# Rewriting the tail of an attention and expert kernel: pointer operands, tables by matmul, rows scattered by register

## Chip, cores, metric

One Trainium2 chip, one core. The metric is the device time of one execution in microseconds (us). Times quoted for a kernel are medians of its runs. Of every run the span (first to last instruction, 1.8 to 2.1 us shorter than the device time) and the mean granted TensorE clock are on record; of one run of each kernel the whole trace is kept, called its profiled run below.

## The reference

LayerNorm, attention with 16 query heads that share one key and one value head, a residual, then a block that picks the 8 rows with the largest routing score, sends those through a gated expert and adds the result back to them.

```python
B, S, D, H, F, C = 1, 2048, 448, 16, 1792, 8
h  = x + softmax(q @ k.T * Dh**-0.5) @ v @ wo          # x normalised by LayerNorm first
xn = layernorm(h)
r  = xn @ w_r                                          # one routing score for each row
idx = argsort(-r)[:8]
y  = (silu(xn[idx] @ w_gate) * (xn[idx] @ w_up)) @ w_down * sigmoid(r[idx])
h2 = h + xn; h2[idx] += y
```

## The kernel before

Each operation is handed to a static scheduler (`G.op(engine, function, assumed ns, reads, writes, ...)`), which works out one fixed order for each engine before the program is built. `DV` is VectorE, `AC` ScalarE, `PO` GpSimd, `PE` TensorE, `SP` SyncE. `port=True` tells the scheduler to keep an operation from running beside GpSimd's operations of the same mark. `urgent`, `prio` and the assumed time steer the order.

The main part runs in 16 blocks of 128 rows. ScalarE computes most exponentials. The rest is shared by VectorE and GpSimd. At the end of each block come small VectorE operations on one value per row:

```python
G.op(DV, lambda e: e.scalar_tensor_tensor(st[:, t, 6:7], mv[:, t, 0:1], -1.0, st[:, t, 4:5],
                                          ALU.mult, ALU.mult), 80,
     reads=[("mv", t), ("st4", t)], writes=[("st6", t)])
# ... (cut)
G.op(DV, lambda e: e.scalar_tensor_tensor(r_col[:, t:t + 1], st[:, t, 6:7], sw[:, 0:1], st[:, t, 2:3],
                                          ALU.mult, ALU.add), 80,
     reads=[("st6", t), "sw", ("st2", t)], writes=[("r", t)], port=True)
```

When 15 of the 16 blocks have their routing scores, the candidates are gathered: 8 from each block, into a row of 120.

```python
G.op(DV, lambda e: e.tensor_copy(rp[:, 0:NT1], r_col[:, 0:NT1]), 80, reads=[...], writes=["rp"])   # the "rp cast"
G.op(PE, mm(ps[0:NT1, VB, 0:128], rp[:, 0:NT1], ident[:, :], True, True), 60, ...)
G.op(DV, lambda e: e.tensor_copy(r16[:, :], ps[0:NT1, VB, 0:128]), 200, ...)
G.op(DV, lambda e: e.max(c8[:, :], r16[:, :]), 200, ...)
dma(crow[0:1, :].rearrange("o (t k) -> o t k", k=8), c8[:, :], ["crow"], reads=["c8"])
G.op(DV, lambda e: e.max_index(i8[:, :], c8[:, :], r16[:, :]), 260, ...)
# ... (cut: row number of each candidate into i8f)
dma(cidx[:, :], i8f[:, :], ["cidx"], reads=["i8f"])
```

The last block and the expert follow. The expert's result is scattered by one indirect DMA. Every engine then loads a flag that says whether the fast path was numerically safe, and branches over a second, exact program:

```python
evs.append(G.op(PO, lambda e: e.indirect_dma_start(out=out[0],
    out_offset=bass.IndirectOffsetOnAxis(ap=idx2[:, 0:1], axis=0), in_=rows8, ...), 1000, ...))

def run(e):                                   # one for each engine
    G.emit(eng, e)
    e.wait_ge(G.flag_sem, G.flag_val)
    bad = e.value_load(flag[0:1, 0:1])
    with e.If(bad != 0):
        ...                                   # the exact program
    if eng == SP:
        for s, v in G.final_waits:
            e.wait_ge(s, v)
```

## Time and profile before

| | before |
|---|---|
| median of 3 runs | 393.55 us (392.94 to 394.22) |
| profiled run: device time, span, mean TensorE clock | 394.32, 392.5, 0.991 |
| last exponential ends | 370.8 us |
| from there to the end of the span | 21.7 us |

### The profile page before, as it was taken

To read this page: it belongs to the slowest core of one execution; us is meant where nothing else is said; L and a number is where in the kernel's file an instruction comes from. 1 tells how busy PE (TensorE), PEld (TensorE's weight loads), DVE (VectorE), ACT (ScalarE), POOL (GpSimd) and SP (SyncE) were. 2 spreads that over 40 slices of the span, in tenths; PEclk is the share of its full clock that TensorE was granted. 3 is DMA by queue.
4 is the path that set the end of the run, shared out by engine and by line. 5 is a ranking of instruction groups with operands and counts; after the bars stand their busy time and mean duration, and the time that the engine had idled before them with its cause. 6 is when DMAs were issued, how large, how long until landed. Compare 5 with 4: busy or idle time off the path is not lost.

```text
span 392.5 us, 8604 instructions
## 1 busy us (share of the span) xinstructions
PE 319.9 (82%) x3501; PEld 110.6 (28%) x3501; DVE 338.5 (86%) x695; ACT 366.7 (93%) x307; POOL 193.4 (49%) x180
## 2 busy tenths in 40 slices
PE   8899887878787888878787878888787878788794
PEld 4454322323232222223231322222232312122242
DVE  6995888989898998989898989989898989879872
ACT  5799999999999999999999999999999999799850
POOL 7410135646555464656365454646563654456410
PEclk9999999999999999999999999999999999799999
DMA  7993000010102010100102010100101020100110
GB/s 210 234 244 86 11 17 15 14 52 4 63 5 63 3 52 13 34 33 5 61 3 65 3 63 4 49 16 29 39 4 62 3 65 3 60 3 3 47 42 10
DMA packets 19892, 17.59 MB, mean 45 GB/s; under 512 B 6326, under 2 KB 17094, under 8 KB 19846
## 3 DMA queue, kind: packets, MB, share of 16 engines
q1 hardware_dynamic: 19781, 16.95, 15.8%
q8 instruction: 30, 0.49, 0.6%
q14 instruction: 17, 0.13, 0.1%
q0 software_dynamic: 64, 0.02, 0.0%
HBM read 11.44 MB, written 5.53 MB: 43 GB/s over the span
## 4 chain that ended last, share of the span: by engine, by line
DVE 60%; PE 23%; ACT 12%; issue 4%; POOL 0%; POOLq 0%
DVE Y L910 28%; PE ps L478 22%; ACT P L885 12%; DVE Y L919 11%; DVE st L752 2%; DVE Q L596 2%; DVE hbuf L730 2%; DVE Ot L932 2%; DVE junk L766 2%; DVE bn L734 2%; DVE bn L609 1%; DVE xnT L653 1%; DVE xx L638 1%; DVE mv L735 1%; DVE K L670 1%
## 5 line engine op out<-in xcount | busy, mean ns | idle before, releaser
L885 ACT ACTIVATE P<-ps 128x1536 bf16<-128x1536 f32 (+1 forms) x281 | 355.2, 1422 | 5.0 <-PE ps L478 4.5
L910 DVE TENSOR_SCALAR Y<-ps 128x512 int16<-128x512 f32 x240 | 164.0, 683 | 32.7 <-PE ps L478 32.6
L921 POOL TENSOR_TENSOR Y<-Y,step 128x1024 int32<-128x1024 int32 x60 | 113.5, 1892 | 142.7 <-DVE Y L919 142.1
L478 PE MATMUL ps<-Q,K 32*128 32x512 bf16 x1024 | 111.5, 385 | 62.6 <-DVE Y L910 45.8
L478 PE MATMUL ps<-Y,Vs 128*32 128x512 bf16 x960 | 89.6, 387 | 2.4 <-DVE Y L919 0.5
L478 PEld LDWEIGHTS ps<-Q,K 32*128 32x128 bf16 x1024 | 33.2, 91 | 177.8 <-ACT P L885 160.2
L919 DVE TENSOR_SCALAR Y<-Y 128x2048 int16<-128x2048 int16 x120 | 82.3, 696 | 0.6
L478 PE MATMUL ps<-P,Vs 128*32 128x512 bf16 x784 | 73.0, 388 | 0.0
L478 PE MATMUL ps<-zero 128*32 128x512 bf16 (+3 forms) x162 | 51.4, 395 | 1.2 <-DVE zero L497 1.2
L478 PEld LDWEIGHTS ps<-Y,Vs 128*32 128x32 bf16 x960 | 23.3, 94 | 33.3 <-issue 17.9
L713 POOL TENSOR_TENSOR On<-Ot,Rb 128x256 bf16<-128x256 f32 x28 | 19.8, 727 | 15.2 <-DMA Rb<-l_scr 15.2
L478 PEld LDWEIGHTS ps<-P,Vs 128*32 128x32 bf16 x784 | 18.8, 94 | 28.7 <-issue 26.7
L738 POOL TENSOR_TENSOR st<-st,nhalf 128x1 f32<-128x1 f32 x15 | 17.8, 1185 | 4.6 <-DVE st L736 4.6
L478 PEld LDWEIGHTS ps<-zero 128*32 128x32 bf16 (+1 forms) x162 | 14.4, 101 | 14.8 <-issue 7.5
L478 PE MATMUL ps<-xnT,wq_pad 112*128 112x128 bf16 x256 | 17.4, 220 | 0.0
L758 POOL TENSOR_SCALAR xx<-hbuf,st 128x448 bf16<-128x448 f32 x15 | 15.6, 1041 | 0.0
L478 PEld LDWEIGHTS ps<-xnT,wq_pad 112*128 112x128 bf16 x256 | 14.4, 98 | 3.6 <-issue 3.4
L478 PE MATMUL ps<-wo_pad,On 128*128 128x448 bf16 x64 | 15.0, 355 | 0.0
L755 POOL TENSOR_SCALAR xx<-hbuf,st 128x448 bf16<-128x448 f32 x15 | 11.2, 746 | 1.6
L730 DVE TENSOR_TENSOR hbuf<-ps,xx 128x448 f32<-128x448 f32 x15 | 9.4, 623 | 2.3 <-PE ps L478 2.3
L596 DVE TENSOR_SCALAR Q<-ps,qone 128x512 bf16<-128x512 f32 x15 | 11.2, 744 | 0.0
L752 DVE SCALAR_TENSOR_TENSOR st<-mv,st 128x1 f32<-128x1 f32 x15 | 11.1, 738 | 0.0
(179 smaller groups left out, 170.1 us busy)
## 6 DMA issues: line engine op xcount, KB each, us to landing
Rb<-l_scr SPq DMA_DIRECT2D x14, 256.0 KB
x_scr<-xx SPq DMA_DIRECT2D x15, 224.0 KB, 2.5
out_dram<-xx SPq DMA_DIRECT2D x16, 112.0 KB, 1.7
wg_sb<-in_B_w_gate_dram SPq DMA_DIRECT2D x1, 1568.0 KB, 14.3
wu_sb<-in_B_w_up_dram SPq DMA_DIRECT2D x1, 1568.0 KB, 20.5
wd_sb<-in_B_w_down_dram SPq DMA_DIRECT2D x1, 1568.0 KB, 25.4
xx<-in_A_x_dram SPq DMA_DIRECT2D x3, 448.0 KB, 5.5
wq_sb<-in_A_wq_dram SPq DMA_DIRECT2D x2, 196.0 KB, 2.9
```

The costliest lines, as they stand in the source:

```text
L478: return lambda e: e.matmul(o, lhsT=l, rhs=r, start=start, stop=stop)
L596: G.op(DV, lambda e: e.tensor_scalar(Q[:, q, :, :].rearrange("p g n -> p (g n)"), ps[:, bank, :], qone[:, 0:1], None, ALU.add), dvt(512), ...
L713: G.op(PO, lambda e, c=c: e.tensor_tensor(On[:, rb, c], Ot[:, rb, c], Rb[:, rb, c], ALU.mult), 750, reads=[both[h], rk[h]], writes=[("On", ...
L730: G.op(DV, lambda e: e.tensor_tensor(hbuf[:, hr, :], ps[:, bank, 0:D], x_sb[:, t, :], ALU.add), dvt(D), reads=[pk(bank), ("x", t)], writes ...
L738: G.op(PO, lambda e: e.tensor_tensor(st[:, t, 4:5], st[:, t, 7:8], nhalf[:, 0:1], ALU.pow), 600, reads=[("st7", t), "nhalf"], writes=[("st ...
L752: G.op(DV, lambda e: e.scalar_tensor_tensor(st[:, t, 6:7], mv[:, t, 0:1], -1.0, st[:, t, 4:5], ALU.mult, ALU.mult), 80, reads=[("mv", t), ...
L755: G.op(PO, lambda e: e.tensor_scalar(outf[:, t, :], hbuf[:, hr, :], st[:, t, 5:6], st[:, t, 6:7], ALU.mult, ALU.add), 800, reads=[("h", hr ...
L758: G.op(PO, lambda e: e.tensor_scalar(xn[:, t, :], hbuf[:, hr, :], st[:, t, 4:5], st[:, t, 6:7], ALU.mult, ALU.add), 800, reads=[("h", hr), ...
L885: G.op(AC, lambda e: e.activation(P[:, s0:s0 + w, :], ps[:, b0:b0 + w, :], ACT.Exp, bias=-(ZERO + SHIFT) * OCT, scale=OCT), w * 427 + 50, ...
L910: G.op(DV, lambda e: e.tensor_scalar(Y[:, y, 0, q, :].bitcast(I16), ps[:, vb, :], 0.0, 32639.0 - STEP[3], ALU.max, ALU.min), dvt(512), rea ...
L919: done = [G.op(DV, lambda e, c=c: e.tensor_single_scalar(y[c].bitcast(I16), y[0].bitcast(I16), STEP[c], ALU.add), 600, reads=r, writes=[(" ...
L921: G.op(PO, lambda e: e.tensor_tensor(y[3].bitcast(I32), y[0].bitcast(I32), step3[:, 0:1].broadcast_to([128, 1024]), ALU.add), 2050, reads= ...
```

## The change

The intent has three parts. The small VectorE operations that read two tensors become `tensor_scalar` with a per-row pointer operand, which is meant to keep GpSimd from holding them (the `st6` operations took 0.738 us each on average before). The two candidate tables are made by a masked multiply and a matmul with ones instead of by two DMAs. The eight result rows are stored by eight DMAs whose row number is in a register, four from SyncE and four from ScalarE, instead of one indirect DMA from GpSimd. With it go a longer assumed time for one matmul group (700 ns, was 250) and the copy of the base rows on ScalarE. The core of the diff (cut: the same rewrite in three more places, set-up of the masks, new reads and writes):

```diff
-        G.op(DV, lambda e: e.scalar_tensor_tensor(st[:, t, 6:7], mv[:, t, 0:1], -1.0, st[:, t, 4:5],
-                                                  ALU.mult, ALU.mult), 80,
+        G.op(DV, lambda e: e.tensor_scalar(st[:, t, 6:7], mv[:, t, 0:1], st[:, t, 4:5], -1.0, ALU.mult, ALU.mult),
+             80,
...
-        dma(crow[0:1, :].rearrange("o (t k) -> o t k", k=8), c8[:, :], ["crow"], reads=["c8"])
+        G.op(DV, lambda e: e.tensor_tensor(spread, bmask, c8[:, :].unsqueeze(1).broadcast_to([NT1, NT1, 8]), ALU.mult),
+             200, reads=["c8", "bmask"], writes=["spread"])
+        G.op(PE, mm(ps[0:1, VB, 0:NC1], onesb[0:NT1, 0:1], wq_sb[0:NT1, 3, 0:NC1], True, True), 60, mode="F",
+             reads=["onesb", "spread"], writes=[pk(VB)])
...
-                  mm(ps[0:8, VB, 26:27], trow[:, 0:8], oneF[:, 0:1], True, True)], 250, mode="F",
+                  mm(ps[0:8, VB, 26:27], trow[:, 0:8], oneF[:, 0:1], True, True)], 700, mode="F",
...
+    def fetch(e, j0):
+        v = None
+        for j in range(j0, j0 + 4):
+            row[j] = e.value_load(idx2[0:1, j:j + 1], min_val=0, max_val=S - 1)
+        return row[j0]
+    loads = [G.op(q, lambda e, j0=j0: fetch(e, j0), 400, reads=["idx2"], writes=[("row", j0)], name="load",
+                  prio=hot + 70) for q, j0 in ((SP, 0), (AC, 4))]
...
-    G.op(DV, lambda e: e.tensor_copy(base8, ps[0:8, 2, 0:D]), 531, reads=[pk(2)], writes=["base8"])
+    post.append(G.op(AC, lambda e: e.activation(base8, ps[0:8, 2, 0:D], ACT.Identity), 480, reads=[pk(2)],
+                     writes=["base8"]))
...
-    evs.append(G.op(PO, lambda e: e.indirect_dma_start(
...
+    for j in range(8):
+        q, ld = (SP, loads[0]) if j < 4 else (AC, loads[1])
+        o = G.op(q, lambda e, j=j: e.dma_start(out[0, bass.ds(row[j], 1), :], rows8[j:j + 1, :]), 60,
...
```

More of the change, by code (lines that the diff above doesn't have):

```diff
@@ L343, in emit @@
             hold = None
-            if w and not o.dma:
+            if w and not o.dma and o.name != "load":
                 hold = w.pop()
@@ L431, in _main @@
     i8 = sb("i8", [NT1, 8], U32)
-    i8f = sb("i8f", [NT1, 8], F32)
     crow = sb("crow", [1, NC1], F32)
     cidx = sb("cidx", [NC1, 1], F32)
+    tbase = sb("tbase", [128, 1], F32)
+    tbi = sb("tbi", [128, 1], I32)
     top8 = sb("top8", [1, 8], F32)
@@ L453, in _main @@
     fin = wq_sb[0:8, 2, 176:180].bitcast(F32)
-    idx2 = wq_sb[0:8, 2, 180:182].bitcast(U32)
+    idx2 = wq_sb[0:1, 2, 180:196].bitcast(I32)
     selb = wq_sb[:, 0, 0:256].bitcast(F32)
@@ L458, in _main @@
     onesb = wq_sb[:, 1, 128:256]
+    spread = wq_sb[0:NT1, 3, 0:NC1].rearrange("p (t k) -> p t k", k=8)
+    bmi = wq_sb[0:NT1, 3, 0:2 * NC1].bitcast(I32)
+    spreadi = wq_sb[0:NT1, 3, 120:120 + NC1].rearrange("p (t k) -> p t k", k=8)
+    bmask = wq_sb[0:NT1, 3, 240:240 + NC1].rearrange("p (t k) -> p t k", k=8)
     wst = sb("wst", [128, 12], F32)
@@ L576, in _main @@
     G.op(PO, lambda e: e.tensor_copy(pcol[:, :], iota_ci[:, 0:1]), 150, reads=["iota_ci"], writes=["pcol"], prio=123)
+    G.op(DV, lambda e: e.tensor_single_scalar(tbi[:, :], iota_ci[:, 0:1], 120, ALU.bitwise_and), 70, reads=["iota_ci"],
+         writes=["tbi"], prio=123)
+    G.op(DV, lambda e: e.tensor_single_scalar(tbase[:, :], tbi[:, :], 16.0, ALU.mult), 70, reads=["tbi"],
+         writes=["tbase"], prio=123)
     G.op(PO, lambda e: e.tensor_copy(rsig[:, 0:1], iota_ci[:, NT - 1:NT]), 150, reads=["iota_ci"], writes=["rs0"],
          prio=123)
-    G.op(PO, lambda e: e.iota(iota_ci[:, 0:8], [[1, 8]], base=0, channel_multiplier=0), 140, reads=["pcol", "rs0"],
+    G.op(PO, lambda e: e.iota(iota_ci[:, 0:8], [[1, 8]], base=0, channel_multiplier=0), 140, reads=["pcol", "rs0", "tbi"],
          writes=["iota_ci"], prio=124)
@@ L582, in _main @@
     G.op(PO, lambda e: e.memset(xselT[:, :, :], 0.0), 250, writes=["xselT", ("wq_sb", 1)], prio=124)
+    G.op(PO, lambda e: e.iota(bmi, [[-1, NT1], [0, 8]], base=0, channel_multiplier=1), 250, reads=["xselT"],
+         writes=["bmask"], prio=124)
+    G.op(PO, lambda e: e.tensor_single_scalar(bmask, bmi.rearrange("p (t k) -> p t k", k=8), 0, ALU.is_equal), 560,
+         reads=["bmask"], writes=["bmask"], prio=124)
     G.op(DV, lambda e: e.tensor_reduce(sw[:, :], w_rb[:, :], AX.X, ALU.add), dvt(D), reads=["w_rb"], writes=["sw"],
@@ L743, in out_proj @@
                  reads=[("h", hr), "w_rb"], writes=["junk", ("st2", t)], port=True, prio=G.prio - 880)
-            G.op(DV, lambda e: e.scalar_tensor_tensor(st[:, t, 3:4], mv[:, t, 0:1], sw[:, 0:1], st[:, t, 2:3],
-                                                      ALU.mult, ALU.subtract), 80,
+            G.op(DV, lambda e: e.tensor_scalar(st[:, t, 3:4], mv[:, t, 0:1], sw[:, 0:1], st[:, t, 2:3],
+                                               ALU.mult, ALU.subtract), 80,
                  reads=[("mv", t), "sw", ("st2", t)], writes=[("st3", t)], **now)
@@ L768, in out_proj @@
              reads=[("h", hr), ("st4", t), "w_rb"], writes=["junk", ("st2", t)], port=True)
-        G.op(DV, lambda e: e.scalar_tensor_tensor(r_col[:, t:t + 1], st[:, t, 6:7], sw[:, 0:1], st[:, t, 2:3],
-                                                  ALU.mult, ALU.add), 80,
-             reads=[("st6", t), "sw", ("st2", t)], writes=[("r", t)], port=True)
+        G.op(DV, lambda e: e.tensor_scalar(r_col[:, t:t + 1], st[:, t, 6:7], sw[:, 0:1], st[:, t, 2:3],
+                                           ALU.mult, ALU.add), 80,
+             reads=[("st6", t), "sw", ("st2", t)], writes=[("r", t)])
     hot = -3000.0
@@ L791, in last_proj @@
              reads=[pk(bank), ("mv", t), "w_rb"], writes=["junk", ("st2", t)], port=True)
-        G.op(DV, lambda e: e.scalar_tensor_tensor(st[:, t, 3:4], mv[:, t, 0:1], sw[:, 0:1], st[:, t, 2:3],
-                                                  ALU.mult, ALU.subtract), 80,
+        G.op(DV, lambda e: e.tensor_scalar(st[:, t, 3:4], mv[:, t, 0:1], sw[:, 0:1], st[:, t, 2:3],
+                                           ALU.mult, ALU.subtract), 80,
              reads=[("mv", t), "sw", ("st2", t)], writes=[("st3", t)])
@@ L798, in last_proj @@
         G.prio = hot + 10
-        G.op(DV, lambda e: e.scalar_tensor_tensor(st[:, t, 6:7], mv[:, t, 0:1], -1.0, st[:, t, 4:5],
-                                                  ALU.mult, ALU.mult), 80,
+        G.op(DV, lambda e: e.tensor_scalar(st[:, t, 6:7], mv[:, t, 0:1], st[:, t, 4:5], -1.0, ALU.mult, ALU.mult),
+             80,
              reads=[("mv", t), ("st4", t)], writes=[("st6", t)])
@@ L948, in stage1 @@
         G.op(DV, lambda e: e.max(c8[:, :], r16[:, :]), 200, reads=["r16"], writes=["c8"])
-        dma(crow[0:1, :].rearrange("o (t k) -> o t k", k=8), c8[:, :], ["crow"], reads=["c8"])
+        G.op(DV, lambda e: e.tensor_tensor(spread, bmask, c8[:, :].unsqueeze(1).broadcast_to([NT1, NT1, 8]), ALU.mult),
+             200, reads=["c8", "bmask"], writes=["spread"])
+        G.op(PE, mm(ps[0:1, VB, 0:NC1], onesb[0:NT1, 0:1], wq_sb[0:NT1, 3, 0:NC1], True, True), 60, mode="F",
+             reads=["onesb", "spread"], writes=[pk(VB)])
         G.op(DV, lambda e: e.max_index(i8[:, :], c8[:, :], r16[:, :]), 260, reads=["r16", "c8"], writes=["i8"])
-        G.op(DV, lambda e: e.tensor_copy(i8f[:, :], i8[:, :]), 70, reads=["i8"], writes=["i8f"])
-        G.op(DV, lambda e: e.scalar_tensor_tensor(i8f[:, :], pcol[0:NT1, 0:1].broadcast_to([NT1, 8]), 128.0, i8f[:, :],
-                                                  ALU.mult, ALU.add), 80, reads=["i8f", "pcol"], writes=["i8f"])
-        dma(cidx[:, :], i8f[:, :], ["cidx"], reads=["i8f"])
+        G.op(DV, lambda e: e.tensor_tensor(spreadi, bmask, i8[:, :].unsqueeze(1).broadcast_to([NT1, NT1, 8]), ALU.mult),
+             200, reads=["i8", "bmask"], writes=["spreadi"])
+        G.op(PE, mm(ps[0:NC1, VB, 128:129], spreadi.rearrange("p t k -> p (t k)"), onesb[0:NT1, 0:1], True, True), 60,
+             mode="F", reads=["onesb", "spreadi"], writes=[pk(VB)])
+        G.op(DV, lambda e: e.tensor_copy(crow[:, :], ps[0:1, VB, 0:NC1]), 200, reads=[pk(VB)], writes=["crow"])
+        G.op(DV, lambda e: e.tensor_tensor(cidx[:, :], ps[0:NC1, VB, 128:129], tbase[0:NC1, :], ALU.add), 80,
+             reads=[pk(VB), "tbase"], writes=["cidx"])
         G.op(DV, lambda e: e.max(top8[:, :], crow[:, :]), 190, reads=["crow"], writes=["top8"])
@@ L1137, in _main @@
     G.op(DV, lambda e: e.tensor_copy(ohf[0:8, 1, :], oh[0:8, 1, :]), 70, reads=["oh1"], writes=["ohf1"])
-    G.op(PE, [mm(ps[0:8, rbank, 0:2], ohf[:, 0, :], rsig[:, :], True, False),
-              mm(ps[0:8, rbank, 0:2], ohf[0:8, 1, :], cols[:, 0:2], False, True)], 200, mode="F",
+    G.op(PE, [mm(ps[0:8, rbank, 0:1], ohf[:, 0, :], rsig[:, 1:2], True, False),
+              mm(ps[0:8, rbank, 0:1], ohf[0:8, 1, :], cols[:, 1:2], False, True),
+              mm(ps[0:1, rbank, 8:16], rsig[:, 0:1], ohf[:, 0, :], True, False),
+              mm(ps[0:1, rbank, 8:16], cols[:, 0:1], ohf[0:8, 1, :], False, True)], 400, mode="F",
          reads=["ohf0", "ohf1", "rs0", "rs1", "cols"], writes=[pk(rbank)])
-    G.op(DV, lambda e: e.tensor_copy(fin[:, :], ps[0:8, rbank, 0:2]), 130, reads=[pk(rbank)], writes=["fin"])
-    G.op(DV, lambda e: e.tensor_copy(idx2[:, :], fin[:, 0:1]), 70, reads=["fin"], writes=["idx2"])
+    G.op(DV, lambda e: e.tensor_copy(fin[:, 0:1], ps[0:8, rbank, 0:1]), 130, reads=[pk(rbank)], writes=["fin"])
+    G.op(DV, lambda e: e.tensor_copy(idx2, ps[0:1, rbank, 8:16]), 130, reads=[pk(rbank)], writes=["idx2"])
+    row = {}
+    def fetch(e, j0):
[5 more added lines that the diff above has]
+                  prio=hot + 70) for q, j0 in ((SP, 0), (AC, 4))]
     G.op(PE, [mm(ps[0:8, 2, 0:D], oh[:, 0, :], outf[:, t, :], True, False),
@@ L1145, in _main @@
          reads=["oh0", "oh1", ("outf", t), "both8"], writes=[pk(2)])
-    G.op(DV, lambda e: e.tensor_copy(base8, ps[0:8, 2, 0:D]), 531, reads=[pk(2)], writes=["base8"])
+    post.append(G.op(AC, lambda e: e.activation(base8, ps[0:8, 2, 0:D], ACT.Identity), 480, reads=[pk(2)],
+                     writes=["base8"]))
     G.prio = hot
-    G.op(DV, lambda e: e.scalar_tensor_tensor(rows8, ps[0:8, dbank, 0:D], fin[:, 1:2], base8, ALU.mult, ALU.add), 540,
+    G.op(DV, lambda e: e.scalar_tensor_tensor(rows8, ps[0:8, dbank, 0:D], fin[:, 0:1], base8, ALU.mult, ALU.add), 540,
          reads=[pk(dbank), "fin", "base8"], writes=["rows8"])
-    evs.append(G.op(PO, lambda e: e.indirect_dma_start(
-        out=out[0], out_offset=bass.IndirectOffsetOnAxis(ap=idx2[:, 0:1], axis=0), in_=rows8, in_offset=None,
-        bounds_check=S - 1, oob_is_err=False), 1000, reads=["rows8", "idx2"] + [("out", k) for k in range(NT)],
-        writes=["scatter"], dma=True))
+    for j in range(8):
+        q, ld = (SP, loads[0]) if j < 4 else (AC, loads[1])
+        o = G.op(q, lambda e, j=j: e.dma_start(out[0, bass.ds(row[j], 1), :], rows8[j:j + 1, :]), 60,
+                 reads=["rows8"] + [("out", k) for k in range(NT)], writes=[("scatter", j)], dma=True)
+        o.deps[ld.idx] = False
+        evs.append(o)
     G.prio = 7000
```

## The prediction

> **What bounds the kernel now.** I read the page first, by engine and by group, then ScalarE's waits stretch by stretch, then the timeline around the one large wait, then the tail by engine.

> The costliest group of the page, and the small VectorE operation that the change rewrites:

> ```profile
> L885 ACT ACTIVATE P<-ps 128x1536 bf16<-128x1536 f32 (+1 forms) x281 | 355.2, 1422 | 5.0 <-PE ps L478 4.5
> L752 DVE SCALAR_TENSOR_TENSOR st<-mv,st 128x1 f32<-128x1 f32 x15 | 11.1, 738 | 0.0
> ```

> ScalarE runs the softmax exponentials 355.2 us of 392.5 and idles only 5.0 us before them. From about 20 to 370.8 us the kernel is ScalarE-bound: time saved on VectorE counts there only where ScalarE waits. ScalarE's waits by stretch: 1.7 us at 14.5 to 20, 1.0 at 20 to 40, 0.3 at 40 to 80, none from 80 to 330, then 2.1 us in one event at 330 to 346. The timeline has its cause:

> ```profile
> 334.44 1.89 POOL L921 TENSOR_TENSOR Y<-Y,step 128x1024 int32<-128x1024 int32 x1
> 334.51 1.85 DVE L752 SCALAR_TENSOR_TENSOR st<-mv,st 128x1 f32<-128x1 f32 x1
> ...
> 336.28 0.68 DVE L910 TENSOR_SCALAR Y<-ps 128x512 int16<-128x512 f32 x1
> ...
> 337.10 0.40 PE L478 MATMUL ps<-Q,K 32*128 32x512 bf16 x4 [2.17 <-DVE Y L910]
> ...
> 337.54 4.04 ACT L885 ACTIVATE P<-ps 128x1536 bf16<-128x1536 f32 x3 [1.35 <-PE ps L478]
> ```

> A one-element operation takes 1.85 us because it ends when GpSimd's 1.89 us operation ends. The next VectorE score tile is late, TensorE waits 2.17 us for it, ScalarE 1.35 us. The windows view shows the after-effect (columns: busy time of PE, PEld, DVE, ACT, POOL with counts, TensorE clock, DMA share, GB/s):

> ```profile
> 330.00:334.50 4.50, 3.77 (x51) 1.08 (x43) 4.39 (x10) 4.50 (x4) 3.17 (x3) 1.00 0.03 5
> 334.50:337.50 3.00, 0.83 (x16) 0.20 (x12) 2.61 (x4) 1.69 (x2) 2.88 (x3) 1.00 0.00 0
> 337.50:345.30 7.80, 7.48 (x55) 1.42 (x59) 5.51 (x11) 6.86 (x6) 2.21 (x2) 0.56 0.25 79
> ```

> TensorE, nearly idle for 3 us, then runs at 0.56 of its clock for 7.8 us, and ScalarE waits 0.50 and 0.23 us more. The event costs 1.35 + 0.50 + 0.23 = 2.08 us. In 13 of the 15 blocks the same operation starts inside that GpSimd operation and ends with it; in twelve it takes about 0.75 us (0.68 in the first) and nothing waits.

> After the last exponential (370.78) the rest, 21.7 us, is a serial chain: accumulator copy, selector matmuls, Ln/Exp, normalise, output projection, LayerNorm and routing on VectorE, expert matmuls, combine, scatter. Any step there counts in full.

> [...]L752 (two inputs) is held, while L750, a 128x1 TENSOR_SCALAR issued 0.06 us before it under the same GpSimd operation, takes 0.14 us in all these blocks. [...]here about 3 us of near idleness led to 0.56. [...]Here one such load takes 0.49 us on SyncE and 0.47 on ScalarE; no run yet shows several in a row.

> **The change part by part.**

> A. Pointer forms, main part. Fifteen `st6` operations become TENSOR_SCALAR with one SBUF tensor and a pointer. A 128x1 TENSOR_SCALAR with a pointer takes 0.21 us (L747, L795); so VectorE saves (0.738 - 0.21) x 15 = 7.9 us, nearly all of it off the bound. What counts is the event: -2.1 us. The fourteen `r` operations (mean 0.222) gain almost nothing.

> B. Candidate tables. The row of 120 candidates leaves by a DMA issued at 369.44, landing 2.0 us later; the index table likewise from 370.52. A masked multiply (estimate 0.25 us from the 0.23 to 0.28 us of its like), a bf16 matmul with its hand-over (0.4) and a PSUM copy (0.24) give the row in about 0.9 us instead. VectorE idles 1.08 us before 371.57, so part of the top-8 search moves there. This chain ends in a gather that is not needed until 380.2, so its own speed is worth nothing. Its VectorE and TensorE work is, because it now sits in front of the critical chain:

> ```profile
> 373.77 0.41 DVE L716 TENSOR_TENSOR On<-Ot,Rb 128x256 bf16<-128x256 f32 x1
> 374.83 0.15 DVE L974 COPY cols<-ps 8x3 f32<-8x3 f32 x1 [0.64 <-PE ps L478]
> 374.91 0.14 DVE L976 COPY bc<-ps 128x8 f32<-128x8 f32 x1
> 374.98 0.40 DVE L716 TENSOR_TENSOR On<-Ot,Rb 128x256 bf16<-128x256 f32 x1
> ```

> The second On has its input at 374.35, yet stands behind two copies that wait for a group of small fp32 matmuls (374.12 to 374.80), which holds up the projection too. The static scheduler of the kernel thought this group took 250 ns; the change tells it 700, near the 0.68 measured. With earlier data and the right length it should put the group elsewhere: -0.6 us.

> C. Pointer forms, tail. `st6` and `st3` of the last block each take a pointer more, 0.06 to 0.1 us, on the serial VectorE chain 376.2 to 380.1: +0.15.

> D. Expert part. The base row copy moves to ScalarE:

> ```profile
> 382.77 0.69 DVE L1123 TENSOR_TENSOR Y<-ps,Y 128x224 bf16<-128x224 f32 x2 [0.62 <-PE ps L478]
> 383.38 0.60 DVE L1146 COPY Y<-ps 8x448 f32<-8x448 f32 x1
> 383.91 0.47 DVE L1127 COPY Y<-ps 112x256 bf16<-112x256 bf16 x2
> ```

> The transposes of the first half end at about 383.5; L1127, which feeds the down projection, starts at 383.91 behind L1146: -0.3 us. The index group becomes eight passes of small fp32 matmuls instead of four, just before the gate projection at 380.96: +0.1. Four register loads enter ScalarE's queue at about 381.4, before the Silu, which starts at 381.94 now. Silu's result has some 0.5 us of slack (ready 382.25, used 382.77). Four loads in series, 4 x 0.47 = 1.9 us, would cost about 1.0; overlapped ones nothing. I take +0.4.

> E. Scatter. Before:

> ```profile
> 387.55 0.67 DVE L1148 SCALAR_TENSOR_TENSOR Y<-ps,wq_sb,Y 8x448 bf16<-8x448 f32 x1 [2.92 <-PE ps L478]
> 389.22 0.92 POOL L1150 DMA_INDIRECT out_dram<-Y,wq_sb  x1 [11.52 <-DVE Y L1148]
> ```

> From the row result (388.22) 1.0 us passes to the start of the indirect DMA, and 2.8 more to its landing (392.0): 3.8 us. After it, each queue issues four DMAs. A DMA issue costs SyncE 0.32 to 0.34 us at best and 0.49 when it has only four rows; with address registers I take 0.45, so the last starts 1.4 us after the rows and lands 1.5 to 1.9 later, at about 3.1. But SyncE now does its end work after its last issue (1.8) rather than beforehand: flag load 0.49, branch 0.05, 0.46 to the first wait, and 24 final waits, two to an instruction at about 0.065, 0.8. That ends at 3.6, with 0.55 us per issue at 4.0. So the landing gains 0.7 and the end about 0: I take 0.0.

> F. Start. Two 0.15 us operations on VectorE and two on GpSimd (0.25, 0.6) fall into idle stretches: 0, or +0.1.

> Sum: -2.1 - 0.6 + 0.15 - 0.3 + 0.1 + 0.4 + 0.0 + 0.05 = -2.3 us; 393.55 - 2.3 = 391.25.

> **Rivals.** (1) The event does not come out, because a pointer read is held like a second tensor, or the rebuilt static schedule makes another of its kind, or it belongs to the profiled run (394.32, above the median 393.55). [...]for the second, that every order in the program is recomputed. Then only -0.2 remains, or +1: 393.3 to 394.5. (2) The register loads run in series before the Silu: -1.7 instead of -2.3, 391.9. (3) The scatter pays in full, because the single-row issues are cheap (0.33) and landing is what ends the run: -0.6 more, 390.6; with the loads hidden too, 390.2.

> **Range and chances.** A is the largest term and has about 0.8 of being real; B and D rest on an order that I have not seen. Together: 391.2, 8 times in 10 between 389.6 and 393.2. Two per cent is 7.9 us, more than everything that the tail could give back, and no part adds as much: within 2% at 0.96.

> **What would show it.** A: L752's successor at about 0.21 us in every block, no ScalarE wait between 80 and 346 us, TensorE clock 1.00 throughout. B: the second On starting within 0.1 us of its Exp. D: L1127 straight behind the transposes, Silu not behind loads. E: time from the row result to the last landing near 3.1 us, but the end of SyncE near 3.8. The prediction is wrong if a wait like that of 334.5 stands elsewhere, or if the tail from 370.8 on is longer than 21 us.

What the terms had besides the traces were estimates: that a pointer read would not be held (A; the trace had for it only L750, 0.14 us beside the GpSimd operation that held L752, and without a pointer), and that register loads might overlap (D, +0.4 between no cost and 1.0). "One such load" is the load of the flag, a register load: 0.490 us on SyncE and 0.467 on ScalarE in the kernel before.

## The result

| | before | after |
|---|---|---|
| median | 393.47 us (4 runs, 392.94 to 394.22) | 399.16 us (4 runs, 398.32 to 399.89) |
| profiled run: device time, span, clock | 394.32, 392.5, 0.991 | 398.32, 396.3, 0.981 |

The changed kernel is slower: ratio 1.0143, 95% interval 1.0116 to 1.0169. A ratio here is the mean time of one kernel's runs over that of the other's of the same rounds, so not quite the ratio of the medians. The result is within 2%, as the prediction gave 0.96 for, but 6 us above its upper end of 393.2.

Where the 3.8 us between the two profiled spans went, by the time from one step to the next:

| stretch | before | after | difference |
|---|---|---|---|
| start to end of the last exponential | 370.77 | 368.28 | -2.49 |
| to the copy of the last accumulator | 0.80 | 1.99 | +1.19 |
| to the LayerNorm statistics of the last block | 4.61 | 6.38 | +1.77 |
| to the gate projection | 4.77 | 5.17 | +0.40 |
| to the Silu | 0.99 | 3.14 | +2.15 |
| to the product of gate and up projection | 0.83 | 0.39 | -0.44 |
| to the down projection | 1.55 | 1.24 | -0.31 |
| to the rows' result | 3.90 | 3.96 | +0.06 |
| to the end | 4.29 | 5.74 | +1.45 |

The main part gained about as predicted, and four places lost more: two before the gate projection, the Silu and the end. The first row alone is good to about 1 us only: the last exponential ends at 366.24 us in the profiled run of ptr_rp and at 367.45 in that of ptr_rp_base, though VectorE, ScalarE and GpSimd do the same in the same order up to there. Below, "rows to end" is the last row of this table.

**The held operation moved.** The group view of the changed kernel (columns: busy us, mean ns) shows the rewritten operation free in all 15 blocks, and two others that are not:

```profile
L765 DVE TENSOR_SCALAR st<-mv,st 128x1 f32<-128x1 f32 x15 | 3.1, 205 | 0.0
L956 DVE CAST rp<-r_col 128x15 bf16<-128x15 f32 x1 | 1.9, 1904 | 0.0
L962 DVE TENSOR_TENSOR wq_sb<-wq_sb,c 15x120 bf16<-15x120 bf16 x1 | 0.5, 537 | 0.0
```

The timeline of the kernel before around its `rp` cast (columns: start, duration, engine, line, operation):

```profile
368.25 0.15 DVE L752 SCALAR_TENSOR_TENSOR st<-mv,st 128x1 f32<-128x1 f32 x1
368.32 0.17 DVE L943 CAST rp<-r_col 128x15 bf16<-128x15 f32 x1
...
368.35 1.89 POOL L921 TENSOR_TENSOR Y<-Y,step 128x1024 int32<-128x1024 int32 x1 [1.53 <-DVE Y L919]
```

and of the changed one at the same place:

```profile
364.15 0.20 DVE L765 TENSOR_SCALAR st<-mv,st 128x1 f32<-128x1 f32 x1
...
364.25 1.89 POOL L934 TENSOR_TENSOR Y<-Y,step 128x1024 int32<-128x1024 int32 x1 [1.53 <-DVE Y L932]
364.27 1.90 DVE L956 CAST rp<-r_col 128x15 bf16<-128x15 f32 x1
...
366.23 0.22 PE L483 MATMUL ps<-ident,rp 128*15 128x128 bf16 x1 [1.61 <-DVE rp L956]
...
366.83 1.45 ACT L898 ACTIVATE P<-ps 128x1536 bf16<-128x1536 f32 x1 [1.11 <-PE ps L483]
```

Before, the cast started 0.03 us ahead of the GpSimd operation and took 0.17 us. Now the operation in front of it takes 0.20 us instead of 0.15, the cast starts 0.02 us behind GpSimd, and takes 1.90. The matmul that reads the cast stands in TensorE's order in front of the score matmuls, and none of these overtakes it in the trace: TensorE waits 1.61 us and ScalarE 1.11.

**The clock fell in the tail.** The windows view of the changed kernel (columns: window, length, busy time of PE, of PEld, which is TensorE's loading of weights, of DVE, ACT, POOL with counts, TensorE clock, DMA share, GB/s):

```profile
364.40:367.82 3.42, 1.21 (x13) 0.36 (x9) 3.04 (x6) 2.31 (x2) 3.14 (x3) 1.00 0.02 8
367.82:378.06 10.24, 9.70 (x41) 4.76 (x42) 4.86 (x22) 2.67 (x8) 1.20 (x1) 0.50 0.12 35
```

and of the kernel before, in about the same work:

```profile
371.57:380.96 9.39, 8.42 (x54) 4.50 (x55) 7.07 (x38) 4.93 (x11) 1.30 (x2) 1.00 0.14 41
```

After the poorly filled stretch the clock is halved for 10.24 us, right where TensorE is on the serial path. That is the +1.77 and, as far as the steps can be told apart, much of the +1.19 and +0.40. The prediction counted on 1.00 throughout.

**The register loads hold the Silu.** Source view of the changed kernel, the line of the loads (columns: duration ns min/median/max, first and last start in us), then the Silu in its timeline:

```profile
L1169 ACTq TENSOR_LOAD <-wq_sb x4: 274/286/467, 382.3 to 384.4; - x4
...
L1169 ACTq FUSED_REGOPS  x4: 147/154/172, 382.8 to 384.7; - x4
```

```profile
384.95 0.60 ACT L1137 ACTIVATE Y<-ps 128x224 f32<-128x224 f32 x2 [3.77 <-PE ps L483]
```

The four loads and their range checks run one after the other, 2.6 us from 382.29 to 384.90, and the Silu, whose input comes with the gate projection of 381.81, starts 0.05 us behind them. The view puts the Silu's wait down to TensorE. It isn't: sequencer work doesn't show as busy, and must be looked up by its line.

**The end.** Source view of the changed kernel, the lines of the row DMAs, the flag load, the flag branch and the closing drain:

```profile
L1183 ACTq DMA_DIRECT2D out_dram<-Y x4: 212/213/523, 390.7 to 392.1; - x4
L1183 SPq DMA_DIRECT2D out_dram<-Y x4: 215/219/323, 390.7 to 392.1; - x4
...
L1248 SPq TENSOR_LOAD <-flag x1: 566/566/566, 392.3 to 392.3; - x1
L1248 ACTq TENSOR_LOAD <-flag x1: 609/609/609, 392.4 to 392.4; - x1
...
L1249 ACTq COMPARE_BRANCH  x1: 45/45/45, 393.0 to 393.0; - x1
...
L1223 ACTq DRAIN  x1: 67/67/67, 396.0 to 396.0; - x1
```

and of the kernel before, its branch and its drains:

```profile
L1216 ACTq COMPARE_BRANCH  x1: 45/45/45, 385.0 to 385.0; - x1
...
L1190 ACTq DRAIN  x1: 81/81/81, 387.7 to 387.7; - x1
...
L1190 POOLq DRAIN  x1: 2220/2220/2220, 390.0 to 390.0; - x1
```

Each of the five engines closes with one drain (L1223 and L1190). Between ScalarE's branch and its drain pass 2.7 us in the kernel before and 2.9 in the changed one. Before, they ran from 385.0 to 387.7, beside the down projection. Now the branch stands behind the row DMAs, and they run from 393.0 to 396.0, to the end of the span (396.29). The rows themselves land earlier than before: the last one 2.76 us after the rows' result (at 393.31), against 3.8.

### The profile page after: what moved, and what is told of

Same layout as the page of the kernel before. It is cut to its first block, busy times and chain, and to the rows that moved or that the text cites. A ratio compares the mean times of both kernels' runs of the same rounds, so it can differ in the third digit from the quotient of the medians.

```text
span 396.3 us, 8661 instructions
## 1 busy us (share of the span) xinstructions
PE 320.8 (81%) x3496; PEld 111.2 (28%) x3499; DVE 335.2 (85%) x698; ACT 365.7 (92%) x308; POOL 193.7 (49%) x181
## 4 chain that ended last, share of the span: by engine, by line
ACT 80%; DVE 9%; PE 6%; DMA 1%; issue 1%; SPq 1%; ACTq 0%; POOL 0%; DVEq 0%
ACT P L898 79%; PE ps L483 6%; DVE bn L622 2%; DMA xx<-in_A_x_dram 1%; DVE xnT L666 1%; DVE Y L923 1%; SPq L509 1%; DVE xx L651 1%; DVE K L683 1%; DVE Y L932 0%; DVE rp L956 0%; ACTq L1169 0%; DVE mv L624 0%; DVE On L729 0%; PE ps L486 0%
## 5 line engine op out<-in xcount | busy, mean ns | idle before, releaser
L483 PE MATMUL ps<-zero 128*32 128x512 bf16 (+3 forms) x151 | 48.7, 402 | 1.6 <-DVE zero L502 1.2
L483 PEld LDWEIGHTS ps<-Y,Vs 128*32 128x32 bf16 x960 | 23.2, 94 | 31.8 <-issue 14.5
L483 PE MATMUL ps<-wo_pad,On 128*128 128x448 bf16 x64 | 15.9, 369 | 0.0
L622 DVE BATCH_NORM_STATS2 bn<-xx 128x6 f32<-128x448 bf16 x16 | 9.8, 612 | 0.6 <-DMA xx<-in_A_x_dram 0.6
```

Source lines behind the costliest of these rows:

```text
L483: return lambda e: e.matmul(o, lhsT=l, rhs=r, start=start, stop=stop)
L622: G.op(DV, lambda e, t=t: e.bn_stats(bn6[:, t, :], x_sb[:, t, :]), dvt(D), reads=[("x", t)], writes=[("bn6", t)])
```

## The experiments

Before's median in the runs shared with the first eight kernels is 393.1 or 393.2 (7 and 8 runs), in the next four 393.3 (11), in the last three 392.73 (11). All results are correct.

**rp_reduce**: the changed kernel with the `rp` cast as a reduction over an axis of one element. Order unchanged.

```diff
-        G.op(DV, lambda e: e.tensor_copy(rp[:, 0:NT1], r_col[:, 0:NT1]), 80,
+        G.op(DV, lambda e: e.tensor_reduce(rp[:, 0:NT1], r_col[:, 0:NT1].unsqueeze(2), AX.X, ALU.max), 80,
```

> The changed kernel with one operation in another form: the cast of the 15 routing columns to bf16, which took 1.90 us beside a GpSimd operation, becomes a reduce over an axis of one element, which writes the same values; the order on every engine stays the same. Theory 1 (the cast stands held by GpSimd, TensorE idles behind it, and its clock is halved in the tail): the operation takes 0.15 to 0.25 us, no ScalarE wait of 1.1 us before the last exponentials, TensorE clock 1.00 from 371 us on, total 3 to 4.5 us less than the changed kernel. Rival 2 (the clock falls in the tail because of the new order there, or of the later length 700): the operation gets short, but only its 1.1 us is gained and the clock stays near 0.5. Rival 3 (the cast waits for its input, the routing columns, and not for GpSimd): it stays long or its start moves, and nothing is gained.

That a reduction would not be held was an estimate of mine: no run before this one shows it. Measured: 396.89 (393.48 to 397.7), ratio 1.0065. The timeline of rp_reduce:

```profile
364.79 1.89 POOL L934 TENSOR_TENSOR Y<-Y,step 128x1024 int32<-128x1024 int32 x1 [1.53 <-DVE Y L932]
364.81 0.16 DVE L956 TENSOR_REDUCE rp<-r_col 128x15 bf16<-128x15 f32 x1
...
365.92 0.90 DVE L962 TENSOR_TENSOR wq_sb<-wq_sb,c 15x120 bf16<-15x120 bf16 x1
...
366.87 0.26 PE L483 MATMUL ps<-wq_sb 15*1 15x120 bf16 x1 [0.97 <-DVE wq_sb L962]
```

The reduction takes 0.16 us under GpSimd's operation of 1.89, where the cast took 1.90, but the same GpSimd operation now holds the first masked multiply of the new tables (two SBUF inputs), TensorE waits 0.97 us for it, and in the profiled run the clock is still halved for 10.24 us. In the change that multiply came later, beside a GpSimd operation of 0.71 us, and took 0.54 us. So there are two held operations in the change, one behind the other, and freeing the first lets the second be held longer. My theory that the cast was the whole of it fell: 2.3 us less than the change by the medians, where I expected 3 to 4.5. One of the four runs took 393.48 us at a mean clock of 0.995, the other three 396.87 to 397.7 at 0.985 or 0.986.

**loads_late**: the changed kernel with ScalarE's register loads behind its base copy.

```diff
     loads = [G.op(q, lambda e, j0=j0: fetch(e, j0), 400, reads=["idx2"], writes=[("row", j0)], name="load",
-                  prio=hot + 70) for q, j0 in ((SP, 0), (AC, 4))]
+                  prio=hot + 70, deps=[post[-1]] if q == AC else ()) for q, j0 in ((SP, 0), (AC, 4))]
```

> The changed kernel with ScalarE's four register loads ordered behind the Silu and the base copy; nothing else moves. Theory 1 (the loads run in series, 0.65 us each with their checks, and hold the Silu): Silu starts 2 to 2.5 us earlier, the gating multiply is back at waiting for TensorE, total 1.6 to 2.0 us less than the changed kernel; the loads then end before the last down-projection matmul and cost nothing. Rival 2 (the Silu waits for the gate projection at the slow clock, and the loads only happen to stand in front): under 0.5 us less.

Measured: 396.64 (396.2 to 397.14), ratio 1.0077. The step to the Silu is 0.99 us again and the next one 0.83, as before. Against the change's 3.14 and 0.39 the loads had cost 1.71 us. The medians differ by 2.5 us, more than I expected, and the two profiled spans by only 1.2; the clock was not the same (mean 0.977 to 0.981 in the change's runs, 0.979 to 0.984 in these), so the steps are the better measure. In this trace the clock is halved for 13.65 us from 365.24 on, only 0.3 us after TensorE began to wait for the held cast.

**scatter_pool**: the changed kernel with the indirect scatter restored, hence no loads.

```diff
-    for j in range(8):
-        o = G.op(q, lambda e, j=j: e.dma_start(out[0, bass.ds(row[j], 1), :], rows8[j:j + 1, :]), 60, ...)
+    evs.append(G.op(PO, lambda e: e.indirect_dma_start(...)))
```

> The changed kernel with the indirect DMA on GpSimd back in place of the register loads and the eight row DMAs. Theory 1 (the loads cost 1.7 us before the multiply and the end costs 1.5 us because ScalarE reaches its flag branch only after its last DMA): 3.0 to 3.4 us less than the changed kernel; from the row result to the end 4.3 us as in the kernel before, against 5.75. Rival 2 (the row DMAs are faster, as intended, and the end is long for another reason such as the slow clock): only the 1.7 us of the loads comes back, and the stretch after the row result is as long as in the changed kernel or longer.

Measured: 394.77 (393.82 to 394.99), ratio 1.0025. Rows to end is 4.31 us; the cast is held 1.90 us and the clock halved for 10.24 us as in the change. The scatter with its loads is the larger half of the loss: 4.4 us by the medians, more than the 3.0 to 3.4 expected, and 3.1 by the profiled spans.

**ptr_only**: the kernel before with the pointer forms alone. The order is the same as before.

> The kernel before with the pointer forms alone. Theory 1 (part A of the prediction holds, and the held cast comes from the shift that this part causes): the state operation takes 0.21 us in every block and the ScalarE wait of 1.35 us near 335 us is gone; if the cast of the routing columns then falls beside a GpSimd operation, most of it is given back in the tail and the total lies within 0.5 us of the kernel before, the clock in the tail down to 0.5; if it does not, the total is 2 to 3 us less than the kernel before. Rival 2 (the held cast comes from the candidate tables or their new length): no held cast here, 2 to 3 us less. Rival 3 (pointer operands are held as second tensors are): the state operation still takes 0.75 us.

Measured: 393.86, but from 391.12 to 396.15 in four runs, ratio 1.0016 (0.9949 to 1.0083). The rewritten operation takes 0.20 us in every block, and nothing waits near 335 us. But the cast starts 0.02 us behind GpSimd and is held 1.90 us with no rebuilt schedule at all: the pointer form's own extra 0.06 us does it. In the profiled run the clock was halved for one stretch only (3.41 us). Of the other runs no trace is kept, but their mean clock is on record, and the times follow it: 391.12 us at 0.998, 392.73 (the profiled run) at 0.995, 395.0 at 0.984, 396.15 at 0.981. So the spread goes with how long the clock was down.

**ptr_rp**: the same with the reduction instead of the cast.

> The kernel before with the pointer forms, and the cast of the routing columns as a reduce over an axis of one element (same order on every engine as in the kernel before). Theory 1 (the pointer forms are worth 2 to 3 us, and the held cast alone ate that up): the cast takes 0.15 to 0.2 us, no ScalarE wait after 80 us, clock 1.00 to the end, 2.5 to 3.5 us less than the kernel before, and a smaller spread of the times than with the pointer forms alone. Rival 2 (the half clock of the tail has another cause): the clock still falls near 366 us and the total is within 1 us of the kernel before.

Measured: 390.10 (389.82 to 390.49, 6 runs), ratio 0.9916 (0.9893 to 0.9939). Windows view of ptr_rp, the stretch in which the change ran at half clock:

```profile
366.00:376.00 10.00, 8.46 (x52) 4.35 (x53) 6.84 (x36) 4.98 (x12) 1.95 (x3) 1.00 0.13 38
```

The clock is 1.00 up to TensorE's last matmul, and the runs agree within 0.7 us. The pointer forms are worth 3.1 us once nothing else is held.

**tables_only**: the kernel before with the tables by matmuls and the 700 ns.

> The kernel before with the candidate tables by masked multiplies and matmuls, and the length 700, alone. Theory 1 (the masked multiply has two SBUF inputs and stands behind the GpSimd operation of that moment, with TensorE's in-order queue behind it): the first masked multiply takes 0.7 to 1.1 us, TensorE idles about 1 us at 369 to 371 us, the clock falls in the tail, 1 to 4 us more than the kernel before. Rival 2 (the prediction's part B: the tables only ease the order of the tail): the multiply takes 0.25 us and the total is 0.5 us less. Rival 3 (the tables' matmuls are slow only because the clock is already down from the held cast): no fall of the clock here, within 0.5 us.

Measured: 396.28 (394.13 to 396.69), ratio 1.0058. Here the cast still precedes GpSimd (0.17 us), the masked multiply takes 0.93 us, TensorE waits 1.00 us, the clock is halved for 6.83 us, and the step from accumulator copy to statistics takes 6.37 us instead of 4.61. So the tables hold TensorE up by themselves. (This kernel has the 700 ns as well; in len700 below these alone gain 0.38 us.)

**scatter_only**: the kernel before with the register loads, the row of indices and the eight row DMAs; base copy on VectorE.

> The kernel before with the register loads, the index row and the eight row DMAs alone. Theory 1 (loads in series before the Silu 1.7 us, and an end 1.4 us later because ScalarE reaches its flag branch late, both apart from the clock): 2.8 to 3.4 us more than the kernel before at a clock of 1.00 in the tail. Rival 2 (the row scatter pays on its own and only looked slow at the half clock): within 0.5 us of the kernel before plus the 1.7 us of the loads, so under 2.2 us more.

Measured: 396.95 (396.89 to 398.07), ratio 1.0098, so some 3.9 us more than before, where 2.8 to 3.4 were expected. Clock 1.00 in the tail up to TensorE's last matmul. The step to the Silu takes 3.14 us, and rows to end 5.37 against before's 4.29: ScalarE's branch at 392.16, its drain at 394.70, span 395.0.

**ptr_rp_base**: ptr_rp with the base copy on ScalarE.

> As ptr_rp, with the copy of the base rows on ScalarE as well. Theory 1 (part D of the prediction: that copy held the first guT copy by 0.3 us): from the gating multiply to the first down-projection matmul 1.24 us in place of 1.55, total 0.3 us less than ptr_rp and 3 to 4 us less than the kernel before. Rival 2 (another wait takes its place there): no change against ptr_rp.

Measured: 390.33 (389.73 to 391.03, 6 runs), ratio 0.9918. The step to the down projection falls from 1.55 to 1.24 us, as predicted; the total does not resolve 0.3 us against ptr_rp.

**len700**: ptr_rp_base with the longer assumed time.

```diff
-                  mm(ps[0:8, VB, 26:27], trow[:, 0:8], oneF[:, 0:1], True, True)], 250, mode="F",
+                  mm(ps[0:8, VB, 26:27], trow[:, 0:8], oneF[:, 0:1], True, True)], 700, mode="F",
```

> This is ptr_rp_base with one scheduling length changed: the group of small fp32 matmuls is declared 700 ns instead of 250. The prediction's step B said that the second On would then no longer stand behind the two copies. Theory (as predicted): the second On starts within 0.1 us of its input, about 0.6 us earlier than in ptr_rp_base, the output projection follows, and the total falls by 0.3 to 0.6 us, to about 389.7 where ptr_rp_base had 390.3. Rival: the static order still puts On behind the copies, or the projection then waits for something else, so the time from the accumulator copy to the LayerNorm statistics stays 4.6 us and the total moves by less than 0.2.

Measured: 389.85 (389.33 to 390.15, 6 runs), ratio 0.9906. Timeline of len700, VectorE:

```profile
370.56 0.43 DVE L716 TENSOR_TENSOR On<-Ot,Rb 128x256 bf16<-128x256 f32 x1 [0.18 <-ACT Rb L708]
371.02 0.15 DVE L974 COPY cols<-ps 8x3 f32<-8x3 f32 x1
```

The second On (the second half of the last block's attention output, normalised) starts 0.03 us after the exponential that it needs (370.53), ahead of the copy that it stood behind, and accumulator copy to statistics takes 4.23 us instead of 4.61: -0.38.

**tables_port**: ptr_rp_base with the tables and the 700 ns, and both masked multiplies declared `port=True`.

```diff
-             200, reads=["c8", "bmask"], writes=["spread"])
+             200, reads=["c8", "bmask"], writes=["spread"], port=True)
```

> This is ptr_rp_base with the candidate tables by matmuls and the 700 length, and with the two masked multiplies declared to the static scheduler as operations that cannot share their access with GpSimd, so that it orders GpSimd's operation around them. Theory (the tables cost because the multiply is held and TensorE then stands still and is halved): the masked multiplies take 0.3 us or less, TensorE has no wait of 0.5 us or more between 362 and 372, its clock is 1.00 to the end, and the total is within 0.6 us of ptr_rp_base (389.7 to 390.9). Rival 1: the extra work of the tables costs of itself: no held operation, clock 1.00, yet over 0.8 us slower than ptr_rp_base. Rival 2: the scheduler's picture of GpSimd is not the chip's, the multiply is held as before and the total is near that of tables_only's cost, 392 to 394.

Measured: 389.55 (389.29 to 390.13, 6 runs), ratio 0.9904. Timeline of tables_port:

```profile
364.01 1.89 POOL L934 TENSOR_TENSOR Y<-Y,step 128x1024 int32<-128x1024 int32 x1 [1.53 <-DVE Y L932]
...
365.42 0.62 DVE L962 TENSOR_TENSOR wq_sb<-wq_sb,c 15x120 bf16<-15x120 bf16 x1
365.97 0.27 DVE L967 TENSOR_TENSOR wq_sb<-wq_sb,i 15x120 bf16<-15x120 bf16 x1
...
366.29 0.35 PE L483 MATMUL ps<-wq_sb 15*1 15x120 bf16 x2
```

The multiply is placed later and is held for some 0.35 us only, until GpSimd's operation ends at 365.90 (0.62 us in all, where I expected 0.3 or less). Its matmul comes after other matmuls, TensorE doesn't wait for it, and the clock stays at 1.00 up to TensorE's last matmul. Last exponential to statistics is 0.91 + 3.85 = 4.76 us, against 5.03 in len700 and 5.41 in ptr_rp_base.

**rp_direct**: the pointer forms, with the routing scores written straight in bf16 where the cast read them, and no cast.

```diff
-            G.op(DV, lambda e: e.tensor_scalar(r_col[:, t:t + 1], st[:, t, 3:4], st[:, t, 4:5], -1.0, ALU.mult,
+            G.op(DV, lambda e: e.tensor_scalar(rp[:, t:t + 1], st[:, t, 3:4], st[:, t, 4:5], -1.0, ALU.mult,
```

> This is the pointer forms alone, with the routing columns written straight in bf16 where the cast read them, and the cast removed, so nothing is left there that GpSimd can hold. Theory: no wait of 1 us or more on ScalarE after 80 us, clock 1.00 to the end, total as ptr_rp's 390.1 or up to 0.3 us less. Rival: the rebuilt static order (one operation fewer) makes another held operation, and the total is 392 or more.

Measured: 390.28 (390.17 to 390.79, 6 runs), ratio 0.9922, clock 1.00 up to TensorE's last matmul. As good as the reduction (390.10), from another order of operations: what counts is that nothing held stands there.

**flag_first**: scatter_only with the flag's load and branch ahead of the row DMAs on SyncE and ScalarE.

```diff
-                G.emit(eng, e)
+                G.emit(eng, e, False)          # all but the row DMAs
                 e.wait_ge(G.flag_sem, G.flag_val)
                 bad = e.value_load(flag[0:1, 0:1])
                 with e.If(bad != 0):
+                    G.emit(eng, e, True)       # the row DMAs
                     ...
+                if eng in (SP, AC):
+                    with e.If(bad == 0):
+                        G.emit(eng, e, True)
```

> This is scatter_only with the flag's register load and branch moved ahead of the row DMAs on SyncE and ScalarE; the rows are then issued last. Theory (ScalarE's end work after its branch, about 2.5 to 2.9 us, hidden before, sets the end because the branch comes after the row DMAs): from the rows' result to the end falls from 5.4 us to between 3.2 and 4.3, and the total by 1 to 2 us, from scatter_only's 397.0 to 395 to 396. Rival: the end work follows the row DMAs whatever comes before it, so ScalarE's end still comes about 2.5 us or more after its last issue, and from rows to end stays at 5.0 or more with the total within 0.4 us of scatter_only.

Measured: 396.04 (394.43 to 397.24, 6 runs), ratio 1.0059. Rows to end fell from 5.37 to 3.83 us, as the theory had it. ScalarE's branch is at 385.56, its next instruction at 388.12, so its 2.5 us lie beside the down projection. But in this profiled run the down projection ran partly at half clock (mean clock 0.67 from 385.17 to 389.90 us): from its start to the rows' result took 5.45 us instead of 3.90. TensorE had stood idle 1.70 us behind the late Silu; in scatter_only it stood idle just as long and kept its clock ("The halved clock" below has what differs). So the total did not isolate the end, and three more runs were made to settle it.

**tables_port_b**: the same kernel as tables_port, as control.

> The same kernel as tables_port, as the control on this chip. Expected: 389.3 to 389.9, rows to end 4.2 us, clock 1.00.

Measured: 389.46 (388.96 to 389.96, 4 runs). Rows to end 4.43 us.

**rows_flag_last**: the control with the eight row DMAs, ScalarE's loads behind the base copy, flag check after the rows.

> tables_port with the eight row DMAs in place of the indirect one, ScalarE's register loads behind its base copy, and the flag check after the row DMAs, as the change has it. Theory (ScalarE's end work after a late branch sets the end): rows to end 5.2 to 5.8 us against the control's 4.2, total 1.0 to 1.6 us above the control. Rival (the surplus of scatter_only came from the loads before the Silu alone): rows to end 4.3 or less, total within 0.3 us of the control.

Measured: 391.31 (391.12 to 391.65, 5 runs), rows to end 5.63 us, clock 1.00 through the down projection. Every other step after the last exponential is within 0.05 us of the control. With nothing else disturbed, the scatter, even with ScalarE's loads moved, costs 1.2 us in the profile and 1.85 in the medians.

**mended**: rows_flag_last with the flag check of flag_first.

> rows_flag_last with the flag check ahead of the row DMAs on both queues. Theory: rows to end 3.5 to 4.0 us, so 0.2 to 0.6 us below the control and 1.4 to 1.9 below rows_flag_last: about 389.2. Rival: the loads and the flag check, all in ScalarE's queue behind the base copy, are not done when the rows are ready, the row DMAs start late by 0.5 us or more, and nothing is gained over the control.

Measured: 392.31 (392.03 to 393.55, 6 runs). The rival came true. Source view of mended: flag branch, the next branch, and the row DMAs of ScalarE:

```profile
L1252 ACTq COMPARE_BRANCH  x1: 45/45/45, 382.2 to 382.2; - x1
...
L1264 ACTq COMPARE_BRANCH  x1: 40/40/40, 384.8 to 384.8; - x1
...
L1185 ACTq DMA_DIRECT2D out_dram<-Y x4: 213/213/2057, 385.6 to 388.6; - x4
```

The rows are ready at 383.45. ScalarE, with its loads late, branches at 382.2 and needs until 384.8 for its next instruction; its first row DMA starts at 385.6 and takes 2.06 us. Rows to end: 6.68. SyncE, past the same branch in 0.46 us, issues its first row at 383.64. The same 2.5 us gap, moved by the order of ScalarE's queue, lay hidden in flag_first and on the path here. Its cause is not settled: the trace has 12 transfers of kind "instruction" from 376 us on, and no run tells whether the gap is a fetch of them. Why the first row DMA took 2.06 us is open as well.

## Why the prediction was wrong

In short: it held that only the rewritten operations could be held and that the clock would stay at 1.00. Instead the cast was held for 1.90 us and the new multiply for 0.54, TensorE stood still behind them, and the clock was halved for 10.24 us of the tail. The register loads cost 1.71 us instead of 0.4, and the scatter's end 1.45 instead of 0.

**A, pointer forms, -2.1.** Right in its mechanism, and a little small: the operation takes 0.205 us in every block as estimated (0.21), and the main part ends 2.49 us earlier (to about 1 us, see above) although 1.11 us were lost again at 366.83. ptr_rp shows the whole worth, 3.1 us by the medians. What failed is "clock 1.00 throughout", and behind it the view that only the rewritten operations could be held. The prediction looked for two-tensor operations; the cast has one input, and in the kernel before, ahead of GpSimd's operation, it took 0.17 us. The cast had 0.03 us to spare and nothing protects it in the scheduler's order. ptr_only and ptr_rp, which share an order with the kernel before, show this to be the effect of 0.06 us, so the rival "another of its kind" was right in its result and wrong in its reason, which was a rebuilt order.

**B, tables, -0.6.** The sign was wrong for the kernel as written, +2.3 us in tables_only. The step that failed is the masked multiply at an "estimate 0.25 us": an operation with two SBUF inputs beside a 1.89 us GpSimd operation is just what part A removes elsewhere, and the prediction worked out its time from free ones. It takes 0.93 us alone, beside that operation, and 0.54 in the change, beside a later one of 0.71 us. Its matmul stands in TensorE's queue, so the statement that the chain's "own speed is worth nothing" failed as well. Free of the hold the estimate holds: 0.38 us by the length (len700) and 0.27 by the tables (tables_port), 0.65 together.

**The halved clock** is in no term of the sum. The prediction read the clock event at 337 us as part of the cost of one wait and did not ask what such a fall costs in the tail, where TensorE is on the path. From the accumulator copy to the statistics the new order takes 6.38 us at half clock and 3.85 at full clock (tables_port). So the fall costs about 2.5 us in that one step, an estimate since the two kernels differ in more than the clock, and the +1.77 is what the gain of part B leaves of it.

The half-clock stretches that end before TensorE's last matmul (3.41, 6.83, 10.24 us, and 13.65 in loads_late) are multiples of 3.41 us, and so are the times between the falls of one trace: in flag_first they are at 337.14, 384.93 and 391.75 us, 14 and 2 times 3.41 us apart. In the changed kernel they are at 367.82 and 391.71, 7 times 3.41 us apart. So the falls of each of these traces fit a fixed grid of windows of 3.41 us. In the windows of the kept traces that ended in a fall before the last matmul, TensorE was busy for 1.08 to 2.14 of 3.41 us. Of those at full clock that ended before the last matmul without a fall, from 40 us on, two had 1.98 and 2.10 us and all others 2.25 or more. This is what parts flag_first (first line) from scatter_only, in the windows view with the columns as above:

```profile
381.52:384.93 3.41, 1.66 (x15) 0.72 (x11) 1.39 (x5) 0.60 (x2) 0.00 (x0) 1.00 0.01 2
383.24:386.65 3.41, 1.98 (x12) 1.00 (x14) 1.82 (x7) 0.61 (x2) 0.00 (x0) 1.00 0.01 2
```

The idle 1.70 us lie within one window in flag_first and are split between two in scatter_only. No run tells why windows of 2.13 and 2.14 us fell (rp_reduce, loads_late) and one of 1.98 did not; matmul ends are modelled, so this is no threshold.

**C, +0.15.** The stretch from the statistics to the gate projection takes 0.06 us more in ptr_rp (4.837 against 4.774), less than half of the estimate.

**D.** The base copy, -0.3: measured -0.31. The index group, +0.1: 0.05 us (scatter_only's 4.82 against 4.77). The loads, +0.4, were mis-sized: they are serial, each is a load of 0.27 to 0.47 us and a range check of 0.15 to 0.17, with gaps between them 2.6 us in all, and cost 1.71. The prediction had weighed loads in series, "4 x 0.47 = 1.9 us" and a cost of about 1.0, its rival 2; that left out the checks and the gaps.

**E, scatter, 0.0.** Right where it looked: landing 0.7 us earlier was predicted, 1.0 measured, and SyncE's work ended 3.8 us after the rows' result, as predicted. Wrong in "the end about 0": it followed SyncE's work after its last issue and forgot that ScalarE, now issuing too, has its own flag load and branch behind its rows, and 2.9 us more after that. Measured +1.45 us in the change, +1.08 in scatter_only, +1.20 in rows_flag_last. The trace of the kernel before had the number: branch at 385.0, drain at 387.7.

**F** is not resolved: block starts differ by more than 0.1 us from run to run.

So the sum had one right large term and four wrong ones (the tables, the clock, the loads, the end), each from work that now comes into contact with a neighbour. The single parts measured alone (ptr_only +0.6, tables_only +2.3, scatter_only +3.9 us from the ratios, the base copy not among them) add up to 6.8, against 5.6 for the whole. The difference is not resolved: the 95% interval of ptr_only alone is 2.6 us to either side.

The best version is tables_port, 389.5 us: pointer forms, the cast as a reduction, tables with the multiply declared, base copy on ScalarE, and the old scatter. Against before that is -1.0% (ratios 0.9904 and, as control, 0.9910). Its lead of 0.3 us over len700 is not resolved by the intervals.

## What to carry to other kernels

When an operation gets slower by 0.05 us ahead of a contested resource, look who follows it and by how much that one made it; and when you remove a held operation, ask of every new operation beside it whether it can be held too. Work that an engine does after its last useful instruction is free only while another engine ends later (ScalarE's 2.7 us after its branch were, its 2.9 us in the change were not): list it before giving that engine the last step. The Silu's wait of 3.77 us, which a view put on TensorE, was for the most part sequencer work here (loads and checks, 2.6 us), which counted as busy nowhere: where a view names an engine that had long been done, look for such work.
